# Forgetting attention and channel mix on one core: new durations for GpSimd's operations and a fixed part per matmul in the planner that orders the instructions

## The chip, the cores and the metric

The kernel runs on one core of one Trainium2 chip. The metric is device time in microseconds, the median over runs. A profiled execution lists every instruction of the five engines: TensorE (PE for its matmuls, PEld for its weight loads), VectorE (DVE), ScalarE (ACT), GpSimd (POOL) and SyncE (SP), which issues nearly all DMAs.

## The reference

Inputs: `q`, `k`, `v` of 8 batches x 8 heads x 576 positions x 64, a gate `s` per head and position, and the weights of a channel mix with `d_model` 512 and `d_ff` 1024. All is float32.

```python
scores = scale * np.matmul(q, k.transpose(0, 1, 3, 2))
cum = np.cumsum(np.maximum(s, 0.0), axis=-1)
bias = -(cum[:, :, :, None] - cum[:, :, None, :])
scores = np.where(causal, -1e9, scores + np.minimum(bias, 0.0))
attn = np.exp(scores - scores.max(-1, keepdims=True))
attn = attn / (attn.sum(-1, keepdims=True) + 1e-09)
x = np.matmul(attn, v)        # heads side by side: (8, 576, 512)
...
xk = mu_k * x + (1.0 - mu_k) * x_prev      # x_prev: x one position earlier
xr = mu_r * x + (1.0 - mu_r) * x_prev
k = np.maximum(xk @ w_k, 0.0)
out = 1 / (1 + np.exp(-(xr @ w_r))) * (k * k @ w_v)
```

## The kernel before, in words

**Attention.** The work goes in 36 visits, each a pair of heads of one batch: batch 0 in two parts (the first three query tiles, then the last two), the batches behind it whole, with four visits each. A visit takes, head by head: score products on TensorE (line 847 for the first 8 visits, in plain float32; line 858 afterwards, where q and k are split into a high and a low part and two products replace the plain one), written to one of two PSUM banks named `s`; a reduction on VectorE (line 875) that adds the causal mask, keeps the row minimum `nm` and writes the scores to `W`; the exponential on ScalarE (line 893) with the row sums in `sums`; on GpSimd a small operation on `rinv` (line 956), on VectorE the reciprocal (line 961); the normalizing on GpSimd (line 912). Then the probabilities are turned: in the first 12 visits by TensorE (lines 1001, 1016), later by 32x32 transposes on VectorE (line 939) and DMAs from `turned` to `ph` (line 1137). The product with v (`po`, lines 975 and 1166) ends a visit, and its result goes to `x_d` in DRAM. GpSimd also makes the split of q and k (`KH`, line 811; `G`, line 815).

**Channel mix.** The 4608 positions are cut into 18 chunks of 256. A chunk mixes x with its predecessor (ScalarE, line 1230; VectorE, line 1241, in the PSUM bank `xp`), splits the result into a high part (ScalarE, line 1261) and a low part `xl` (VectorE, line 1263), and multiplies: the hidden products with `w_k` (line 1308), the gate with `w_r` (line 1359) and the output with `w_v` (line 1390). They accumulate in one of two PSUM banks named `m`, which the eviction `g` on VectorE (line 1400) sets free at the end of an output. Chunk 0 multiplies in plain float32; afterwards each product is done three times (high x high, low x high, high x low).

**Weights.** They arrive as 64-bit floats, 20 blocks of 128 x 512. ScalarE and four operations on VectorE (lines 678, 685, 689, 696) convert a block, in the banks `m` and `xp`. The two banks `m` are given out in turn: first to the blocks of `w_k` and `w_r`, then to the hidden products of chunk 0 and what follows. On GpSimd a cast (line 709) and a subtraction (line 714) then split it into the high and low halves `wr_k`, `wr_r`, `wr_v`.

**What sets the order.** The program is first recorded as 7652 tasks (class `Plan`); then a planner orders them. Each task names its engine, a duration in ns, the buffers it reads and writes, and a due time. `Plan.forward` runs a list scheduling: of the tasks that are ready on an engine it takes the one with the earliest due time (on TensorE, VectorE and ScalarE out of the next few). `Plan.backward` gives new due times from the result; 40 such passes are made, and the order of the pass with the earliest planned end is written out, engine by engine. Inside an engine that order is fixed; between engines, semaphores hold it. While TensorE has nothing to do before the first chunk, `forward` puts in filler matmuls on the identity (line 447). The durations come from small helpers: `pe` for TensorE takes the columns times a rate, `pool` for GpSimd the elements per partition times a rate plus a constant `extra` that the caller gives (36 for a memset, 114 for the casts and the subtraction to `G`, 94 for line 714, 100 for line 956, 244 for line 912).

```python
def pe(emit, reads, writes, n, m=P, cycle=1.0625 / 2.4, k=P, land=None):
    i = plan.add("PE", n * cycle, emit, reads, writes, land=land or 0.83 * m + 1)
...
def pool(emit, reads, writes, n, extra, rate=0.8333):
    return plan.add("POOL", n * rate + extra, emit, reads, writes)
...
if name != "v":                       # load_weight: a block of w_k or w_r
    ps = bank(1, "m", 2)
...
return bank(1, "m", 2)                # product_bank: the sums of a chunk
...
order, _, _, emits = best
for n, i in enumerate(order):
    for emit in emits.get(n, ()):
        emit()
    self.tasks[i][2]()
```

Of the kernel before, what the change touches and what calls it, by code (L numbers as in the profile page):

```python
# [337 lines left out]
def forgetting_attention_then_channel_mix(  # L338
# [38 lines left out]
    plan = Plan()  # L377
# [13 lines left out]


    def pe(emit, reads, writes, n, m=P, cycle=1.0625 / 2.4, k=P, land=None):
        i = plan.add("PE", n * cycle, emit, reads, writes, land=land or 0.83 * m + 1)
        plan.columns[i] = n * k / P * (4 if cycle > 1 else 1)
        if m == 64 and n > 190 and cycle < 1:
            plan.spare.add(i)
        return i
# [27 lines left out]
    def dve(emit, reads, writes, n, rate=0.96, ports=None):  # L426
        i = plan.add("DVE", n / rate + 68, emit, reads, writes)
        plan.side(i, ports)
        return i

    def pool(emit, reads, writes, n, extra, rate=0.8333):
        return plan.add("POOL", n * rate + extra, emit, reads, writes)

    def aside(emit, reads, writes, ns):
        return plan.add("SP", 1, emit, reads, writes, land=1300 + ns)
# [86 lines left out]
    def blanks():  # L522
        u = turned_d.get()
        for h in range(2):
            a, step = slots(h, 0, 0), slots(h, 1, 1) - slots(h, 0, 0)
            pool(
                lambda a=a, step=step: nc.gpsimd.memset(
                    u[:, 2:4, a : a + step * (NQ - 1) + 1 : step], 0.0
                ),
                [], [(turned_d, (h, t)) for t in range(NQ)], 64 * NQ, 36,  # L530
            )
            pool(
                lambda a=a: nc.gpsimd.memset(u[64:P, 0:2, a : a + 1], 0.0), [], [(turned_d, (h, 0))], 64, 36,
            )

    def zero(t):
        for kb in range(NQ):
            pool(
                lambda kb=kb: nc.gpsimd.memset(t.get()[64:P, col(kb, P * kb) : col(kb, P * kb) + 64], 0.0),
                [], [(t, ("h", kb))], 64, 36,  # L540
            )
# [292 lines left out]
    def scores(b, h, tiles, blocks, G, G2, KH, KL):  # L834
# [7 lines left out]
        def products(t, m, i, k0, w, W):  # L842
            ps = bank(1, "s", 2)
            q0 = QS[t] - QS[tiles[0]]
            if G2 is None:
                pe(
                    lambda: nc.tensor.matmul(
                        ps.get()[:, :w],
                        G.get()[0:65, h % 2, q0 : q0 + P],
                        KH.get()[0:65, h % 2, k0 : k0 + w],  # L850
                        start=True,
                        stop=True,
                    ),
                    [(y, (h % 2, r)) for y in (G, KH) for r in range(2)], [ps], w, P, 4 / 2.4,
                )
            for x, (g, K) in enumerate(((G, KH), (G2, KL)) if G2 is not None else ()):
                pe(
                    lambda x=x, g=g, K=K: nc.tensor.matmul(  # L858
                        ps.get()[:m, :w],
                        g.get()[: 64 + PIECES if x else P, h % 2, q0 : q0 + m],  # L860
                        K.get()[: 64 + PIECES if x else P, h % 2, k0 : k0 + w],
                        start=x == 0,
                        stop=x == 1,
                    ),
                    [(g, (h % 2, 0)), (K, (h % 2, 0))]
                    + ([(g, 1), (K, (h % 2, 2))] if x else [(g, (h % 2, 1)), (K, (h % 2, 1))]), [ps], w, m,
                )
# [123 lines left out]
    def weighted(pts, V, xT, tiles, blocks, hp):  # L991


        def transposed(pt, ph):
# [3 lines left out]
            def turn(ps, place, t, k0, m):  # L998

                pe(  # L1000
                    lambda: nc.tensor.transpose(
                        ps.get()[0:m, place : place + P].bitcast(F32R),
                        piece(pt[t].at[0], pt[t].at[1] + lead(t) + k0, m),
                        ident_r.ap,
                    ),
                    [(pt[t], i) for i in range(3)] + [ident_r], [ps], P, m, land=TURN,
                )
# [618 lines left out]
```

## Time and profile before

| | us |
|---|---|
| median of 3 runs | 796.99 (794.56 to 801.29) |
| the profiled execution's own time | 794.9 |
| its span, first to last instruction | 793.1 |
| TensorE busy | 772.1 |
| VectorE busy | 556.1 |
| ScalarE busy | 467.8 |
| GpSimd busy | 344.2 |

The profiled execution is one run; the span is its time without what lies around the instructions. Matmuls are pipelined, and their recorded durations overlap, so busy time of TensorE says that there was a matmul under way and not that it ran at its peak; the distance from one matmul to the next says more. An idle time that a row shows in brackets is followed by the engine and line that ended it.

### The profile page before, as it was taken

To read this page: it belongs to the slowest core of one execution; us is meant where nothing else is said; L and a number is where in the kernel's file an instruction comes from. 1 tells how busy PE (TensorE), PEld (TensorE's weight loads), DVE (VectorE), ACT (ScalarE), POOL (GpSimd) and SP (SyncE) were. 2 spreads that over 40 slices of the span, in tenths; PEclk is the share of its full clock that TensorE was granted. 3 is DMA by queue.
4 is the path that set the end of the run, shared out by engine and by line. 5 is a ranking of instruction groups with operands and counts; after the bars stand their busy time and mean duration, and the time that the engine had idled before them with its cause. 6 is when DMAs were issued, how large, how long until landed. Compare 5 with 4: busy or idle time off the path is not lost.

```text
span 793.1 us, 15958 instructions
## 1 busy us (share of the span) xinstructions
PE 772.1 (97%) x5115; PEld 634.6 (80%) x5115; DVE 556.1 (70%) x1860; ACT 467.8 (59%) x1305; POOL 344.2 (43%) x616
## 2 busy tenths in 40 slices
PE   7989999999999999999999999999999999999998
PEld 5657767888787878788788888887888788888997
DVE  5989885578766877676687677768877787355521
ACT  3987887766654765474564567456655666345420
POOL 6748999743633444441344434343444421000000
PEclk8999999999999999999999999999999999999999
DMA  6898855688898998898689888889888776421000
GB/s 182 238 293 219 241 152 156 163 214 210 229 234 215 236 230 209 220 250 207 176 201 238 208 221 226 217 232 224 230 229 218 179 198 169 115 75 41 14 27 27
DMA packets 64068, 150.00 MB, mean 189 GB/s; under 512 B 14078, under 2 KB 25604, under 8 KB 63984
## 3 DMA queue, kind: packets, MB, share of 16 engines
q1 hardware_dynamic: 63824, 148.82, 72.6%
q8 instruction: 40, 0.66, 0.4%
q14 instruction: 44, 0.36, 0.1%
q10 hardware_dynamic: 160, 0.16, 0.1%
HBM read 50.29 MB, written 18.43 MB: 87 GB/s over the span
## 4 chain that ended last, share of the span: by engine, by line
PE 44%; DVE 14%; DMA 13%; SPq 11%; POOL 7%; ACT 5%; issue 5%; DVEq 0%; POOLq 0%; ACTq 0%
SPq L1137 11%; PE m L1308 11%; PE m L1390 9%; DMA ph<-turned 4%; DVE turned L939 4%; PE s L858 4%; DMA x<-x_d 4%; PE m L1359 4%; PE po L1166 3%; POOL W L912 3%; DVE W L875 3%; DVE xp L1241 3%; ACT xp L1230 2%; PE s L1390 2%; POOL G L815 2%
## 5 line engine op out<-in xcount | busy, mean ns | idle before, releaser
L893 ACT ACTIVATE W<-W,nm 128x448 f32<-128x448 f32 (+4 forms) x320 | 178.7, 559 | 71.8 <-DVE nm L875 68.2
L1308 PE MATMUL m<-xh,wr_k 128*128 128x256 f32 x960 | 185.1, 282 | 1.6 <-DVE g L1400 1.0
L912 POOL TENSOR_SCALAR W<-W,rinv 128x192 f32<-128x192 f32 (+4 forms) x320 | 164.6, 530 | 26.4 <-DVE rinv L961 24.9
L875 DVE CUSTOM_DVE_ANT_0 W<-s,causal 128x448 f32<-128x448 f32 (+5 forms) x320 | 129.6, 417 | 48.3 <-PE s L858 42.5
L1390 PE MATMUL m<-wr_v,kh 128*128 128x512 f32 (+1 forms) x480 | 159.4, 393 | 0.0
L1308 PEld LDWEIGHTS m<-xh,wr_k 128*128 128x128 f32 x960 | 153.6, 190 | 4.1 <-DVE kl L1345 1.5
L939 DVE STREAM_TRANSPOSE turned<-W 128x64 f32<-128x64 f32 (+5 forms) x432 | 121.9, 327 | 33.5 <-DMA ph<-turned 20.3
L1308 PE MATMUL m<-xl,wr_k 128*128 128x256 f32 x480 | 136.2, 284 | 0.0
L858 PE MATMUL s<-KH,G 128*64 128x64 f32 x336 | 105.0, 325 | 4.5 <-DVE nm L875 4.0
L956 POOL TENSOR_SCALAR rinv<-sums 128x5 f32<-128x5 f32 (+2 forms) x72 | 17.0, 236 | 212.9 <-ACT W L893 206.6
L1230 ACT ACTIVATE xp<-x,mu 128x256 f32<-128x256 f32 (+3 forms) x160 | 66.8, 417 | 67.0 <-DMA x<-x_d 39.7
L1390 PEld LDWEIGHTS m<-wr_v,kh 128*128 128x128 f32 x480 | 89.2, 188 | 15.1
L858 PE MATMUL s<-KL,G 67*64 67x64 f32 x336 | 98.3, 296 | 0.0
L1390 PE MATMUL m<-wr_v,kl 128*128 128x512 f32 (+1 forms) x240 | 94.1, 392 | 0.0
L1308 PEld LDWEIGHTS m<-xl,wr_k 128*128 128x128 f32 x480 | 91.4, 190 | 0.9
L1241 DVE SCALAR_TENSOR_TENSOR xp<-x,mu,xp 128x256 f32<-128x256 f32 (+3 forms) x160 | 64.8, 405 | 34.6 <-ACT xp L1230 32.4
L1359 PE MATMUL m<-wr_r,xh 128*128 128x512 f32 x240 | 81.4, 399 | 0.7 <-DVE kl L1345 0.6
L858 PEld LDWEIGHTS s<-KH,G 128*64 128x64 f32 x336 | 60.3, 180 | 23.3 <-DVE nm L875 14.3
L815 POOL TENSOR_TENSOR G<-raw,KH 128x1152 fp32r<-128x1152 f32 x28 | 74.6, 2665 | 1.8
L1166 PE MATMUL po<-ph,V 128*64 128x64 f32 (+4 forms) x768 | 67.2, 327 | 1.6 <-DMA ph<-turned 1.2
L858 PEld LDWEIGHTS s<-KL,G 67*64 67x64 f32 x336 | 60.4, 180 | 9.1 <-issue 3.0
L1166 PEld LDWEIGHTS po<-ph,V 128*64 128x64 f32 x768 | 39.7, 137 | 27.4 <-issue 23.3
(141 smaller groups left out, 1287.3 us busy)
## 6 DMA issues: line engine op xcount, KB each, us to landing
ph<-turned SPq DMA_DIRECT2D x384, 120.0 KB
raw<-in_q SPq DMA_DIRECT2D x28, 576.0 KB
G<-KH SPq DMA_DIRECT2D x56, 288.0 KB
V<-in_v SPq DMA_DIRECT2D x32, 320.0 KB
out<-g SPq DMA_DIRECT2D x35, 256.0 KB
x_d<-xT SPq DMA_DIRECT2D x28, 288.5 KB
KL<-G SPq DMA_DIRECT2D x28, 288.0 KB
KH<-KH SPq DMA_DIRECT2D x28, 288.0 KB
```

The source lines that it names most:

```text
L815: lambda: nc.gpsimd.tensor_tensor(out=G.get(), in0=x.get(), in1=f32(KH.get()), op=ALU.subtract),
L858: lambda x=x, g=g, K=K: nc.tensor.matmul(ps.get()[:m, :w], g.get()[: 64 + PIECES if x else P, h % 2, q0 : q0 + m], K.get()[: 64 + PIECES i ...
L875: lambda a=a, e=e, at=at, i=i: nc.vector.tensor_tensor_reduce(out=W.ap[:m, at : at + e - a], in0=ps.get()[:m, a - k0 : e - k0], in1=causal ...
L893: lambda: nc.scalar.activation(W.ap[:m, :n], W.ap[:m, :n], AF.Exp, bias=nm.get()[:m, 3 * t + mi : 3 * t + mi + 1], scale=-1.0, accum_out=s ...
L912: lambda: nc.gpsimd.tensor_scalar(out=to(), in0=W.ap[:m, :n], scalar1=rinv.get()[:m, t : t + 1], scalar2=1.0, op0=ALU.mult, op1=ALU.mult,),
L939: lambda a=a, e=e, g=g, n=n: nc.vector.transpose(at(a, e, g), W.ap[:m, P * a : P * a + n].rearrange("p (k g x) -> p k g x", g=g, x=32),),
L1137: lambda g=g, i=i: nc.sync.dma_start(across.get()[32 * g : 32 * g + 32, i], turned_d.get()[32 * i : 32 * i + 32, g]),
L1166: nc.tensor.matmul(to, V.get()[:, kb, j], x, start=ps is rest or kb == 0, stop=ps is rest or kb == NQ - 1 or t == NQ - 1, skip_group_check ...
L1241: lambda n=n, o=o, i=i, to=to: nc.vector.scalar_tensor_tensor(out=x_out.get()[:, c, o : o + n] if plain else to(), in0=x.get()[:, c, o + i ...
L1308: lambda u=u, f=f, c=c, n=n, y=y, x=x: nc.tensor.matmul(ps.get()[:, u * CT : (u + 1) * CT], y[:, f % 4 * P : (f % 4 + 1) * P], x.get()[:, ...
L1359: lambda c=c, n=n, x=x, y=y: nc.tensor.matmul(ps.get(), x.get()[:, c, ts], y, start=c == 0 and n == 0, stop=c == NC - 1 and n == products - 1,
L1390: lambda f=f, n=n, x=x, y=y, ps=ps, ms=ms: nc.tensor.matmul(ps.get()[:, :m], x.get()[:, f, ts], y[:, ms], start=f == 0 and n == 0, stop=f ...
```

## The change

The planner's duration of a matmul, of whatever size, gets 4.5 ns more, and four of the constants of GpSimd's operations are replaced by larger ones: 36 by 90, 94 by 140, 100 by 218, 114 by 165. The durations set nothing but the order.

```diff
@@ -391,7 +391,7 @@
-        i = plan.add("PE", n * cycle, emit, reads, writes, land=land or 0.83 * m + 1)
+        i = plan.add("PE", n * cycle + 4.5, emit, reads, writes, land=land or 0.83 * m + 1)
...
@@ -428,8 +428,10 @@
+    POOL_MORE = {36: 90, 94: 140, 100: 218, 114: 165}
+
     def pool(emit, reads, writes, n, extra, rate=0.8333):
-        return plan.add("POOL", n * rate + extra, emit, reads, writes)
+        return plan.add("POOL", n * rate + POOL_MORE.get(extra, extra), emit, reads, writes)
```

Lines behind 430 have a number larger by two afterwards. Three places of the new order follow, before and after each.

VectorE's queue before the first product of chunk 0, before the change. `w_r_2` and `w_k_3_1` are weight blocks, `m0` and `m1` the two PSUM banks in which they are converted, `W_0` and `W_1` the scores of the two heads, `nm` their row minima, `s0` and `s1` the score banks:

```order
L689 SCALAR_TENSOR_TENSOR m0_218<-w_r_2_0_128,m0_218 128x512
L875 ISA W_1_1024_576_82,nm1_241<-s1_213,causal_95,nm1_241 128x224
L875 ISA nm1_241 128x1
L696 SCALAR_TENSOR_TENSOR w_r_2_0_128<-w_r_2_0_128,m0_218 128x512
L875 ISA W_1_1024_576_82,nm1_241<-s1_213,causal_95,nm1_241 128x64
L875 ISA nm1_241 128x1
L678 TENSOR_SCALAR m1_401<-m1_401 128x512
L685 TENSOR_SCALAR m1_401<-m1_401 128x512
L961 RECIPROCAL rinv1_304<-rinv1_304 128x2
L689 SCALAR_TENSOR_TENSOR m1_401<-w_k_3_1_122,m1_401 128x512
L875 ISA W_0_576_448_76,nm0_226<-s0_216,causal_95 128x448
L875 ISA nm0_226 128x1
```

The same stretch of VectorE's queue after the change:

```order
L698 SCALAR_TENSOR_TENSOR w_k_3_1_122<-w_k_3_1_122,m1_248 128x512
L687 TENSOR_SCALAR m0_217<-m0_217 128x512
L877 ISA W_0_576_448_76,nm0_228<-s0_215,causal_95 128x448
L877 ISA nm0_228 128x1
L963 RECIPROCAL rinv1_305<-rinv1_305 128x2
L691 SCALAR_TENSOR_TENSOR m0_217<-w_r_2_0_128,m0_217 128x512
L877 ISA W_0_1024_576_77,nm0_228<-s1_213,causal_95 128x288
L877 ISA nm0_228 128x1
L680 TENSOR_SCALAR m1_248<-m1_248 128x512
L877 ISA W_0_1024_576_77,nm0_228<-s0_215,causal_95,nm0_228 128x224
L877 ISA nm0_228 128x1
L698 SCALAR_TENSOR_TENSOR w_r_2_0_128<-w_r_2_0_128,m0_217 128x512
```

The last step of `w_r_2` now stands behind `w_k_3_1` and behind three reductions of the next visit's scores.

GpSimd's queue where the low halves of the weights `wr_r` are made, before the change (`rinv0` belongs to head 0 of the visit, `W_0` is what is normalized with it):

```order
L838 MEMSET sums1_179 128x1
L714 TENSOR_TENSOR wr_r_0_0_125<-w_r_0_0_124,wr_r_0_0_125 128x512
L714 TENSOR_TENSOR wr_r_1_0_127<-w_r_1_0_126,wr_r_1_0_127 128x512
L1559 MEMSET xT0_763 128x1
L714 TENSOR_TENSOR wr_r_2_0_129<-w_r_2_0_128,wr_r_2_0_129 128x512
L956 TENSOR_SCALAR rinv0_273<-sums0_167 128x5
L709 CAST wr_v_1_0_135<-w_v_1_0_134 128x512
L838 MEMSET sums0_167 128x1
L714 TENSOR_TENSOR wr_r_3_0_131<-w_r_3_0_130,wr_r_3_0_131 128x512
L912 TENSOR_SCALAR W_0_64_192_74<-W_0_64_192_74,rinv0_273 128x192
L912 TENSOR_SCALAR W_0_256_320_75<-W_0_256_320_75,rinv0_273 128x320
L912 TENSOR_SCALAR W_0_576_448_76<-W_0_576_448_76,rinv0_273 128x448
```

The same stretch of GpSimd's queue after the change (`KH1` is the high part of the q and k of a later visit):

```order
L958 TENSOR_SCALAR rinv0_272<-sums0_168 128x5
L840 MEMSET sums1_180 128x1
L716 TENSOR_TENSOR wr_k_3_1_123<-w_k_3_1_122,wr_k_3_1_123 128x512
L914 TENSOR_SCALAR W_0_64_192_74<-W_0_64_192_74,rinv0_272 128x192
L914 TENSOR_SCALAR W_0_256_320_75<-W_0_256_320_75,rinv0_272 128x320
L914 TENSOR_SCALAR W_0_576_448_76<-W_0_576_448_76,rinv0_272 128x448
L914 TENSOR_SCALAR W_0_1024_576_77<-W_0_1024_576_77,rinv0_272 128x576
L914 TENSOR_SCALAR W_0_192_64_298<-W_0_0_64_73,rinv0_272 64x64
L840 MEMSET sums0_168 128x1
L711 CAST wr_v_1_0_135<-w_v_1_0_134 128x512
L813 CAST KH1_908<-raw1_154 128x1152
L716 TENSOR_TENSOR wr_r_0_0_125<-w_r_0_0_124,wr_r_0_0_125 128x512
```

The normalizing of head 0 moves ahead of all four `wr_r` blocks, the last of which stands 14 places later than before.

VectorE's queue at the end of a chunk (388 us in the trace of before), before the change. `g1` is the eviction that frees a bank `m`, `xp0` and `xl10` the mixing and the low part of the next chunk, `turned` the transposes of attention:

```order
L1263 TENSOR_TENSOR xl10_1364<-xp0_162,xh10_1356 128x512
L939 STREAM_TRANSPOSE turned_90<-W_1_576_448_81 128x3x4x32
L939 STREAM_TRANSPOSE turned_90<-W_1_1024_576_82 128x4x4x32
L1400 SCALAR_TENSOR_TENSOR g1_1195<-g1_1195,m0_218 128x512
L939 STREAM_TRANSPOSE turned_90<-W_1_256_320_80 128x2x32
L939 STREAM_TRANSPOSE turned_90<-W_1_576_448_81 128x2x32
L939 STREAM_TRANSPOSE turned_90<-W_1_1024_576_82 128x2x32
L1241 SCALAR_TENSOR_TENSOR xp0_162<-x0_1201,mu1_92,xp0_162 128x256 x2
```

The same place after the change:

```order
L1265 TENSOR_TENSOR xl10_1304<-xp0_161,xh10_1296 128x512
L1243 SCALAR_TENSOR_TENSOR xp0_161<-x0_1193,mu1_92,xp0_161 128x256 x2
L963 RECIPROCAL rinv1_305<-rinv1_305 128x5
L941 STREAM_TRANSPOSE turned_90<-W_1_64_192_79 128x4x32
L1265 TENSOR_TENSOR xl10_1304<-xp0_161,xh10_1296 128x512
L941 STREAM_TRANSPOSE turned_90<-W_1_0_64_78 64x2x32
L941 STREAM_TRANSPOSE turned_90<-W_1_64_192_79 128x2x32
L941 STREAM_TRANSPOSE turned_90<-W_1_256_320_80 128x2x4x32
L1402 SCALAR_TENSOR_TENSOR g1_1181<-g1_1181,m0_217 128x512
```

The two large transposes now follow the eviction, and the next mixing steps with their low part stand ahead of it.

## Rows read from the trace of the kernel before

**Rows 1.** The page: busy time, share and count of each engine.

```profile
PE 772.1 (97%) x5115; PEld 634.6 (80%) x5115; DVE 556.1 (70%) x1860; ACT 467.8 (59%) x1305; POOL 344.2 (43%) x616
```

**Rows 2.** Sums by stretch: length, busy (count) per engine, clock, DMA share, GB/s.

```profile
0.00:60.00 60.00, 52.18 (x296) 35.56 (x297) 49.60 (x173) 42.46 (x152) 36.00 (x94) 0.91 0.82 239
60.00:160.00 100.00, 99.20 (x637) 74.18 (x636) 73.61 (x264) 79.06 (x245) 90.43 (x132) 1.00 0.69 186
160.00:680.00 520.00, 511.42 (x3508) 429.00 (x3507) 388.03 (x1344) 306.23 (x827) 217.74 (x390) 1.00 0.85 215
```

**Rows 3.** Sums by stretch, two of the 20 us stretches.

```profile
40.00:60.00 20.00, 17.51 (x95) 11.11 (x96) 18.00 (x58) 16.17 (x52) 8.85 (x17) 0.91 0.96 296
...
380.00:400.00 20.00, 18.06 (x113) 16.37 (x112) 14.76 (x45) 11.22 (x28) 5.98 (x12) 0.91 0.69 181
```

**Rows 4.** The chain that ended last: start us, length us, what.

```profile
51.33 3.49 PE po L975 x20
...
63.42 1.89 PE po L975 x20
...
733.62 2.81 PE m L1308 x24
...
750.41 5.54 PE m L1390 x24
```

**Rows 5.** GpSimd's instructions by line: count, duration in ns as min/median/max.

```profile
L956 POOL TENSOR_SCALAR rinv<-sums x72: 223/236/253, 13.6 to 672.9; 128x5 f32<-128x5 f32 x56, 128x3 f32<-128x3 f32 x8, 128x2 f32<-128x2 f32 x8
...
L811 POOL CAST KH<-raw x28: 1134/1144/1151, 61.0 to 626.4; 128x1152 fp32r<-128x1152 f32 x28
...
L815 POOL TENSOR_TENSOR G<-raw,KH x28: 2628/2667/2690, 62.7 to 627.6; 128x1152 fp32r<-128x1152 f32 x28
...
L714 POOL TENSOR_TENSOR wr_k<-w_k,wr_k x8: 1272/1274/1290, 68.9 to 95.0; 128x512 fp32r<-128x512 f32 x8
```

**Rows 6.** Timeline before 60 us: start us, length us, engine, line, [idle before <-releaser].

```profile
18.45 1.27 PE L447 MATMUL xp<-ident 128*128 128x256 bf16 x10
...
51.17 0.68 DVE L696 SCALAR_TENSOR_TENSOR w_r<-w_r,m 128x512 int32<-128x512 int32 x1
...
56.02 0.60 PE L1308 MATMUL m<-xh,w_k 128*128 128x256 f32 x2
...
57.69 0.45 DVE L875 CUSTOM_DVE_ANT_0 W<-s,causal,nm 128x224 f32<-128x224 f32 x1 [0.67 <-PE s L847]
```

**Rows 7.** Timeline: the last low halves of two weights, and chunk 1's first readers.

```profile
95.05 1.29 POOL L714 TENSOR_TENSOR wr_k<-w_k,wr_k 128x512 fp32r<-128x512 f32 x1
...
103.81 1.29 POOL L714 TENSOR_TENSOR wr_r<-w_r,wr_r 128x512 fp32r<-128x512 f32 x1
...
127.78 0.35 PE L1308 MATMUL m<-xh,wr_k 128*128 128x256 f32 x1
...
154.52 0.39 PE L1359 MATMUL m<-wr_r,xh 128*128 128x512 f32 x1
```

**Rows 8.** Timeline of TensorE, 389 to 393 us.

```profile
389.53 0.39 PE L1308 MATMUL m<-xh,wr_k 128*128 128x256 f32 x1 [1.02 <-DVE g L1400]
...
392.45 0.74 PE L858 MATMUL s<-KH,G 128*128 128x448 f32 x1 [0.81 <-DVE nm L875]
```

**Rows 9.** Timeline of VectorE and ScalarE, 387 to 391 us.

```profile
387.18 0.65 DVE L1263 TENSOR_TENSOR xl<-xp,xh 128x512 fp32r<-128x512 f32 x1
387.76 1.14 DVE L939 STREAM_TRANSPOSE turned<-W 128x384 f32<-128x384 f32 x2
388.83 0.64 DVE L1400 SCALAR_TENSOR_TENSOR g<-g,m 128x512 f32<-128x512 f32 x1
...
387.86 0.99 ACT L1230 ACTIVATE xp<-x,mu 128x256 f32<-128x256 f32 x2 [0.77 <-DVE xl L1263]
...
390.81 0.59 ACT L1261 CAST xh<-xp 128x512 fp32r<-128x512 f32 x1 [1.96 <-DVE xp L1241]
```

**Rows 10.** Timeline of TensorE near 292 us.

```profile
292.68 0.42 PE L858 MATMUL s<-KH,G 128*128 128x320 f32 x1 [0.70 <-DVE nm L875]
```

## The prediction

> **What bounds the kernel now.** I read the page's busy line first, then the sums by stretch, then the time from one matmul to the next, then the waits that TensorE itself shows.
>
> TensorE is busy 772.1 us of 793.1 [rows 1]. By stretch the missing 21 us lie in three places [rows 2]: 7.8 us before 60 us (60.00 less 52.18), 0.8 us from 60 to 160, 8.6 us from 160 to 680. That leaves 3.8 us behind 680, most of it the last eviction and store. GpSimd is the fullest engine beside it, but in one stretch alone: 90.43 of 100 us from 60 to 160; afterwards it has 217.74 of 520 [rows 2].
>
> The clock is part of the bound. The granted clock was 0.91 in 40 to 60 and again in 380 to 400 [rows 3], which is 1.8 us of 20 lost each time, so a part of each stretch ran at 1.2 GHz in place of 2.4. What it does to one stage stands in two rows of the same 20 matmuls: 3.49 us at 51.33, 1.89 us at 63.42 [rows 4], so a fall costs about 1.6 us.
>
> A busy TensorE runs close to its rate: 24 matmuls of 256 columns took 2.81 us (117.1 ns each), 24 of 512 columns 5.54 us (230.8 ns) [rows 4]. The planner had 113.3 and 226.7 ns; with 4.5 ns more it has 117.8 and 231.2. So the new constant for TensorE is right within 1 ns, and the old one was 3 % short on the small ones. For GpSimd the traced medians are 236 ns (the small scalar operation on rinv), 1144 (cast to KH), 2667 (the subtraction to G), 1274 (the subtraction of a weight block) [rows 5]; the planner had 102 to 104, 1074, 2660, 1226 and now has 220 to 222, 1125, 2711, 1272. Three of these four come much nearer, G's goes from 7 ns short to 44 ns over.
>
> **The change part by part.** No instruction of the computation is added, removed or altered; the planner's list scheduling gives another order. About half of TensorE's instructions stand at another place, the largest move is 49 places, and what runs behind 695 us stands in the same order on every engine. On TensorE 8 of 75 filler matmuls on the identity go, a count from the two orders. So the sum is one of waits, made against the profiled execution's own 794.9 us.
>
> *Fillers.* Ten of them took 1.27 us at full clock [rows 6], so eight are 1.0 us. They stand in the first 30 us, where TensorE waits for VectorE anyway, so part of this turns into waiting. Bounds −1.0 and 0; I take −0.5.
>
> *The start of the channel mix.* The first product of chunk 0 writes to a PSUM bank that the conversions of the weight blocks use before it; on that bank the block w_r_2 is last. Before, its last step began at 51.17 and took 0.68, and the product came at 56.02 behind other work [rows 6]. In the new order that step stands behind the conversion of w_k_3_1 and three score reductions, the last of which began at 57.69 in the trace of before, after a wait of 0.67 for TensorE [rows 6]; the bank then comes free near 58.7, or near 58.0 without that wait. The product is thus 2.0 to 2.7 us late. The cover is TensorE's own: score products and transposes of the next visits now stand ahead of it. Bounds −1.0 (that work, started sooner, also saves waits) and +2.7 (no cover); nearest to the covered case, since in the row of 56.02 the product already took turns with that work, +0.4.
>
> *GpSimd from 66 to 148 us.* The normalizing of probabilities and the splits of q and k move ahead of the low halves of the weights. The last wr_k low half began at 95.05, the last wr_r one at 103.81; their readers, chunk 1's products, began at 127.78 (wr_k) and 154.52 (wr_r) [rows 7], so delays of about 5 and 10 us are hidden by 30 and 50 us of slack. The gain is bounded by TensorE's whole idle time there, 0.8 us [rows 2], a loss would need a delay of 30 us or more. Bounds −0.8 and 0, I take −0.2.
>
> *The bank at the chunk starts, at 388 us.* TensorE waited 1.02 us at 389.53 for the eviction g on VectorE, and 0.81 us at 392.45 for a reduction behind it [rows 8], and the clock fell there [rows 3]. VectorE's eviction ran at 388.83 behind two transposes of 1.14 us together [rows 9]. In the new order it loses these two, but the next two mixing steps and their subtraction (xl) stand ahead of it. With the times of before: subtraction done at 387.83; ScalarE's two steps 387.86 to 388.85; the two mixing steps end near 389.35; ScalarE's cast (0.59) lets the second subtraction start near 390.0; it and three small transposes take 1.35; the eviction would end at 392.0 instead of 389.47. That is +2.5 us; upstream, four transposes (0.9 us) leave the front of the chain, so less is likelier. Bounds −1.0 (the wait goes) and +2.5 (nothing upstream helps); I take +1.0. Queued behind this eviction are transposes and score reductions of attention, whose products stand among other work of TensorE.
>
> *One wait that is filled.* At 292.68 the score product waits 0.70 us for VectorE [rows 10]. Three output products stood between it and the scores before; now five do. Two more are 0.46 us; bounds −0.7 and 0, taken −0.5.
>
> *The other waits from 160 to 680*, 8.6 less 1.0, 0.8 and 0.7, or about 6 us, are drawn anew. A truer TensorE duration tells the planner that results of other engines come earlier in terms of matmuls, so readers move closer to their producers: less cover. Truer GpSimd durations move its readers away: more cover. I take 0, with half of the 6 us on either side.
>
> The sum is −0.5 + 0.4 − 0.2 + 1.0 − 0.5 = +0.2, or 795.1 us on the profiled execution. The three runs shown have a median 2.1 us above that execution (796.99, from 794.56 to 801.29), so no change would read as 795.9, halfway, for this forecast and the rivals; with +0.2 that is 796. About 1 %, 8 us, is what a measurement of this kernel can tell from no change.
>
> **The clock, for and against.** The rows show a fall at 0.91 in 380 to 400, where TensorE was still busy 18.06 of 20 us and its longest recorded waits were 1.02 and 0.81 us [rows 3, 8]. The Trainium skill (TensorE: Matmul & The Clock Gate, section "What's actually happening") says that the lower clock is the default, that activity lifts it and that an idle stretch lets it fall; this speaks against removing fillers. By the strict form of that rule, waits of about 1 us would never bring a fall, and the slower case below would lose its clock part of 1.6; the trace disagrees, as the fall at 392 stands behind such waits alone.
>
> **Rivals.** *The truer numbers pay everywhere.* Half of the 8.6 us from 160 to 680 goes (4.3), the fall near 392 with it (1.6), and a third of the 7.8 us before 60 (2.6): −8.5, or 787.4. For it speaks that GpSimd is the fullest engine from 60 to 160 and that its small operation on rinv was planned at less than half of its 236 ns [rows 5]. Against it: GpSimd's stage costs TensorE 0.8 us only, and of the two waits shown in [rows 8] both are for VectorE, whose durations do not change. Chance 0.17.
>
> *Slower: evictions late at the chunk starts.* The mechanism is the one at 388 us, at several places. In the new order eleven evictions before 600 us have more of VectorE's work ahead of them than before, by 0.1 to 1.6 us at the traced durations, and eleven have less. If three of them cost what the worked case has as its upper end (2.5) and one more clock fall joins (1.6) they give +9.1, or 805. It decides where the eviction comes later than the products of the bank before it last, 24 of 117 ns or 2.8 us. Against it: only one such wait of TensorE stands out before. Chance 0.14.
>
> *The change does not do what it says.* The order behind 160 us is close to the old one, so the waits stay as they are, with the fillers alone gone: 795.4. This lies inside the forecast's band and I give it 0.24; the forecast proper has 0.45.
>
> **How the numbers follow.** Faster by over 1 % (under 788) is the first rival, 0.17; slower by over 1 % (over 804) the second, 0.14; the rest is 0.69. The range reaches from the first rival's value, 787, to 804, just short of the second's: it leaves out half of the first rival's chance below and most of the second's above, about 0.2 in all. The forecast's own bounds, −1.0 − 1.0 − 0.8 − 1.0 − 0.7 − 3.0 and +2.7 + 2.5 + 3.0, make −7.5 and +8.2 if all fell one way, 788 to 804, which lies in the same range.
>
> **What would show it.** Right: TensorE busy near 771 us and its idle time from 160 to 680 still 6 to 11 us; first product of chunk 0 at 57 to 59 us; the wait at the score product near 292 under 0.3 us; an eviction wait of over 1.5 us near 389. GpSimd's durations within 2 % of the old ones and 90 us busy again in 60 to 160. Wrong: an idle time of TensorE from 160 to 680 under 4.5 us or over 14, one clock fall more or one less than the two of [rows 3], or a chunk 1 that waits for wr_k or wr_r.

## The result and the profile after

The changed kernel took 803.65 us (median of 20 runs, 798.98 to 814.85) beside 797.89 us for the kernel before on the same chips (20 runs, 790.24 to 806.84). The ratio is 1.0087, 95% interval 1.0063 to 1.0112: slower by 7 us by this ratio, by 5.8 between the medians. The forecast of 796 and no change was wrong, though the time lies just inside its range. Twenty runs resolve a quarter of a per cent here; the 1 per cent that the prediction took as the limit was too coarse.

The profiled execution after is one of the quickest of the new kernel, as the one before was of the old: 798.98 us, span 797.2 against 793.1. Its busy line and its sums by stretch (length, busy and count per engine, clock, DMA share, GB/s), with the stretch behind 680 us:

```profile
PE 772.1 (97%) x5107; PEld 632.4 (79%) x5107; DVE 561.1 (70%) x1860; ACT 467.5 (59%) x1305; POOL 344.5 (43%) x616
```

```profile
0.00:60.00 60.00, 52.21 (x298) 34.82 (x299) 53.35 (x183) 44.84 (x160) 38.89 (x98) 0.94 0.77 236
60.00:160.00 100.00, 100.00 (x644) 75.04 (x643) 74.90 (x263) 76.74 (x239) 90.81 (x134) 1.00 0.70 191
160.00:680.00 520.00, 507.37 (x3457) 424.38 (x3457) 387.01 (x1331) 305.50 (x823) 214.71 (x384) 0.99 0.85 213
680.00:798.00 118.00, 112.54 (x714) 98.16 (x710) 45.82 (x86) 40.46 (x84) 0.10 (x1) 1.00 0.18 50
```

TensorE is busy for the same 772.1 us as before [rows 1]. Beside [rows 2] its idle time is unchanged before 60 us (7.8), falls by 0.8 from 60 to 160 (to nothing), rises by 4.0 from 160 to 680 (from 8.6 to 12.6) and by 0.8 behind that (117.2 less 112.54, against 3.8). That is +4.0, and the spans differ by 4.1. So what these two executions show of the loss lies in the steady stage, as waits of TensorE; of the 7 us of the ratio they show 4.1. The waits that it shows itself from 160 to 680 us (who waits, for whom: us, times, longest), first of the kernel before, then after:

```profile
PE s L858 <- DVE nm L875: 4.0, 8, 0.9
PE m L1308 <- DVE g L1400: 1.0, 1, 1.0
...
PE m L1308 <- DVE kl L1345: 0.6, 3, 0.2
```

```profile
PE s L860 <- DVE nm L877: 8.8, 13, 1.8
PE m L1310 <- DVE kl L1347: 1.8, 3, 0.8
```

A score product (s) that waits until VectorE has reduced (nm) the scores that its bank held before: 4.0 us became 8.8. The wait for an eviction (g) is gone. The longest of these waits, in TensorE's timeline after:

```profile
293.16 0.42 PE L860 MATMUL s<-KH,G 128*128 128x320 f32 x1 [1.85 <-DVE nm L877]
...
341.56 0.25 PE L860 MATMUL s<-KH,G 128*64 128x64 f32 x1 [0.97 <-DVE nm L877]
...
381.81 0.40 PE L860 MATMUL s<-KH,G 128*128 128x288 f32 x1 [1.36 <-DVE nm L877]
...
502.44 0.42 PE L860 MATMUL s<-KH,G 128*128 128x320 f32 x1 [1.08 <-DVE nm L877]
...
503.31 0.47 PE L860 MATMUL s<-KH,G 128*128 128x448 f32 x1 [0.32 <-DVE nm L877]
...
536.61 0.42 PE L860 MATMUL s<-KH,G 128*128 128x320 f32 x1 [0.55 <-DVE nm L877]
...
661.59 0.41 PE L860 MATMUL s<-KH,G 128*128 128x320 f32 x1 [0.96 <-DVE nm L877]
```

Why the reduction is late stands in VectorE's own queue. In front of the first of these waits, in the timeline of VectorE:

```profile
290.67 0.96 DVE L1243 SCALAR_TENSOR_TENSOR xp<-x,mu,xp 128x256 f32<-128x256 f32 x2
292.29 0.69 DVE L1265 TENSOR_TENSOR xl<-xp,xh 128x512 fp32r<-128x512 f32 x1 [0.65 <-ACT xh L1263]
292.89 0.20 DVE L877 CUSTOM_DVE_ANT_0 W<-s,causal 64x64 f32<-64x64 f32 x1
```

and the score product that this reduction reads, in TensorE's:

```profile
289.59 0.19 PE L860 MATMUL s<-KH,G 128*64 128x64 f32 x1
```

The scores were there before 290 us. The reduction came at 292.89, behind two mixing steps and the subtraction xl, for which VectorE stood 0.65 us idle until ScalarE's cast was done. The order inside an engine's queue is fixed, so a ready reduction waits behind a mixing chain that is not. At 381 us the picture is the same; at 341 and 661 us it is a mixing step alone, for which VectorE stood idle for 1.64 and 0.91 us until ScalarE's part of it was done; at 502 it is transposes and a subtraction.

Behind 40 us the clock fell twice again, at other places: not in 40 to 60 or 380 to 400, as in [rows 3], but here:

```profile
40.00:60.00 20.00, 17.95 (x103) 11.98 (x104) 19.91 (x63) 17.65 (x56) 10.85 (x20) 1.00 0.87 275
340.00:360.00 20.00, 18.84 (x134) 15.50 (x133) 16.09 (x59) 14.55 (x42) 9.63 (x16) 0.91 0.85 217
380.00:400.00 20.00, 18.64 (x127) 16.89 (x127) 15.50 (x49) 11.83 (x31) 7.88 (x15) 1.00 0.66 170
500.00:520.00 20.00, 18.60 (x118) 15.43 (x118) 12.95 (x47) 8.15 (x25) 7.57 (x12) 0.91 0.81 199
```

Some executions run disturbed, on whatever kernel; the ratios leave them out, and as the profiles of e2, e7 and e13 are of such executions, their rows are not compared.

### The profile page after: what moved, and what is told of

It reads as the page before. It is cut to its first block, busy times and chain, and to the rows that moved or that the text cites. A ratio compares the mean times of both kernels' runs of the same rounds, so it can differ in the third digit from the quotient of the medians.

```text
span 797.2 us, 15944 instructions
## 1 busy us (share of the span) xinstructions
PE 772.1 (97%) x5107; PEld 632.4 (79%) x5107; DVE 561.1 (70%) x1860; ACT 467.5 (59%) x1305; POOL 344.5 (43%) x616
## 4 chain that ended last, share of the span: by engine, by line
PE 52%; SPq 12%; DVE 11%; DMA 11%; ACT 7%; issue 4%; POOL 3%; DVEq 0%; POOLq 0%; ACTq 0%
PE m L1310 14%; SPq L1139 11%; PE m L1392 11%; PE s L860 6%; PE m L1361 4%; DMA x<-x_d 4%; DVE turned L941 4%; PE po L1168 3%; DVE xp L1243 2%; ACT xp L1232 2%; ACT W L895 2%; PE po L977 2%; PE s L1392 2%; DMA KH<-KH 2%; DVE xl L1265 2%
## 5 line engine op out<-in xcount | busy, mean ns | idle before, releaser
L1392 PE MATMUL m<-wr_v,kh 128*128 128x512 f32 (+1 forms) x480 | 161.2, 398 | 0.0
L860 PE MATMUL s<-KL,G 67*64 67x64 f32 (+1 forms) x336 | 99.2, 299 | 0.0
L860 PEld LDWEIGHTS s<-KL,G 67*64 67x64 f32 (+1 forms) x336 | 61.0, 182 | 9.2 <-issue 3.2
L1322 ACT ACTIVATE r<-m 128x512 f32<-128x512 f32 x64 | 38.1, 595 | 40.9 <-PE m L1310 37.7
```

What stands on the lines that cost most here:

```text
L860: lambda x=x, g=g, K=K: nc.tensor.matmul(ps.get()[:m, :w], g.get()[: 64 + PIECES if x else P, h % 2, q0 : q0 + m], K.get()[: 64 + PIECES i ...
L1392: lambda f=f, n=n, x=x, y=y, ps=ps, ms=ms: nc.tensor.matmul(ps.get()[:, :m], x.get()[:, f, ts], y[:, ms], start=f == 0 and n == 0, stop=f ...
```

## The experiments

All ratios are to the kernel before, run beside it on the same chip. The diff of e4 is against the kernel before, all others are against the changed kernel. A changed number makes the planner give another order; such an order is called a draw here. Three theories at first: the longer matmul costs (1), GpSimd's numbers cost (2), any redraw of the order costs or gains by chance (3).

**The two halves alone.** e1 is the change without GpSimd's numbers, e2 the change without the matmul's.

```diff
-    POOL_MORE = {36: 90, 94: 140, 100: 218, 114: 165}
+    POOL_MORE = {}
```

> The kernel before with the 4.5 ns per matmul alone; GpSimd's durations as in the kernel before. Theory 1 (the longer matmul in the plan is what costs; readers of VectorE's results are placed with nothing to spare): as slow as the whole change, a ratio to before of 1.006 to 1.012, TensorE idle from 160 to 680 us 11 to 14 us (before 8.6, after 12.6). Theory 2 (GpSimd's numbers do it): 0.997 to 1.003 and 7 to 10 us. Theory 3 (any new number draws the order anew, the sign is chance): anywhere from 0.993 to 1.012, with waits at other places than in the changed kernel.

```diff
-        i = plan.add("PE", n * cycle + 4.5, emit, reads, writes, land=land or 0.83 * m + 1)
+        i = plan.add("PE", n * cycle, emit, reads, writes, land=land or 0.83 * m + 1)
```

> The kernel before with GpSimd's new durations alone; the matmul as in the kernel before. Theory 1: no loss behind 160 us, a ratio of 0.995 to 1.002 (the start may keep the 3 us that the changed kernel had won by then). Theory 2: 1.006 to 1.012, with 11 to 14 us of idle TensorE from 160 to 680. Theory 3: anywhere from 0.993 to 1.012.

Measured: e1 1.0204 (1.0153 to 1.0256), twice the loss of the whole change; e2 1.0006 (0.9964 to 1.0049). Theory 2 falls. Of e1 the sum of the steady stage, and the largest single wait met in this study, on four engines:

```profile
160.00:680.00 520.00, 494.97 (x3364) 415.38 (x3363) 374.95 (x1296) 297.55 (x801) 213.15 (x381) 0.99 0.85 209
```

```profile
540.00 0.59 SPq L1424 DMA_DIRECT2D x<-x_d  x1
540.63 6.34 SPq L1139 DMA_DIRECT2D ph<-turned  x10
```

```profile
544.26 0.78 ACT L1232 ACTIVATE xp<-x,mu 128x192 f32<-128x192 f32 x2 [5.35 <-DMA x<-x_d]
```

```profile
545.07 0.42 DVE L1243 SCALAR_TENSOR_TENSOR xp<-x,mu,xp 128x192 f32<-128x192 f32 x1 [4.43 <-ACT xp L1232]
545.98 0.29 DVE L1243 SCALAR_TENSOR_TENSOR xp<-x,mu,xp 128x64 f32<-128x64 f32 x1 [0.49 <-ACT xp L1232]
546.18 0.21 DVE L877 CUSTOM_DVE_ANT_0 W<-s,causal 64x64 f32<-64x64 f32 x1
```

```profile
546.45 0.63 PE L860 MATMUL s<-KH,G 128*128 128x320 f32 x1 [5.69 <-DVE nm L877]
```

Read from the top: SyncE issues the load of x at 540.00; ScalarE mixes at 544.26 when it has landed; VectorE has stood idle for 4.43 us with its mixing step at the head of its queue; the reduction behind that starts at 546.18, and TensorE, which has waited 5.69 us for it, goes on. TensorE is idle for 25.0 us of the 520.

**The late reductions moved ahead.** e3 keeps the changed kernel's order but for nine reductions (task numbers of the plan: what is moved, and in front of what); a merge of the engines' queues writes the instructions.

```diff
+    MOVES = ((3122, 2580), (3126, 2580), (4020, 3232), (4174, 3471), (4178, 3471),
+             (5651, 5174), (5655, 5174), (6867, 6326), (6871, 6326))
...
         order, _, _, emits = best
+        order = self.moved_up(order)
```

> The changed kernel's own order, with nine score reductions moved ahead in VectorE's queue at five places (near 291, 340, 380, 501 and 660 us), in front of the mixing steps, the subtraction or the transposes behind which they stood; every other engine's order is untouched. The waits of TensorE in front of score products there are 1.85, 0.97, 1.36, 1.08 with 0.32, and 0.96 us, 6.5 us together, and the clock fell behind two of them. If these waits are the loss: 4 to 7 us less than the changed kernel, a ratio to before of 0.999 to 1.004, and both falls of the clock gone. If the lost time is only passed on (the mixing comes later and TensorE waits for it instead): 1.007 to 1.011, as the changed kernel.

Measured: 1.0041 (1.0009 to 1.0073), between the two expectations; its interval overlaps that of the changed kernel, so in time up to half of the loss may have come back. The profiled execution shows none of that. The same places, some 5 us later in this execution:

```profile
298.80 0.40 PE L882 MATMUL s<-KH,G 128*128 128x288 f32 x1 [1.57 <-DVE nm L899]
...
347.64 0.36 PE L882 MATMUL s<-KH,G 128*128 128x192 f32 x1 [2.74 <-DVE nm L899]
...
508.24 0.40 PE L882 MATMUL s<-KH,G 128*128 128x288 f32 x1 [0.76 <-DVE nm L899]
...
540.25 0.41 PE L882 MATMUL s<-KH,G 128*128 128x320 f32 x1 [1.89 <-DVE nm L899]
...
668.22 0.40 PE L882 MATMUL s<-KH,G 128*128 128x288 f32 x1 [0.25 <-DVE nm L899]
```

The wait near 381 is gone, those near 502 and 661 are shorter by 0.6 and 0.7, but the one at 341 grew from 0.97 to 2.74, and the one near 537, at which nothing was moved, from 0.55 to 1.89. In sum these are 7.2 us against 7.1. At 347 us VectorE stood idle with a mixing step at the head of its queue, and the next reduction stood behind that:

```profile
346.08 1.07 DVE L1265 SCALAR_TENSOR_TENSOR xp<-x,mu,xp 128x64 f32<-128x64 f32 x3 [2.74 <-ACT xp L1254]
347.06 0.51 DVE L899 CUSTOM_DVE_ANT_0 W<-s,causal,nm 128x288 f32<-128x288 f32 x1
```

So in this execution the lost time is passed on along VectorE's queue; whether repairing single places returns a part of it in time stays open.

**Redraws that carry no knowledge.** e4, e5 and e18 change the old matmul by a tenth or two of a nanosecond, with GpSimd's old numbers.

```diff
-        i = plan.add("PE", n * cycle, emit, reads, writes, land=land or 0.83 * m + 1)
+        i = plan.add("PE", n * cycle + 0.1, emit, reads, writes, land=land or 0.83 * m + 1)
```

> A control: the kernel before with 0.1 ns per matmul, a number that carries no knowledge, but moves 1317 of TensorE's instructions by up to 43 places. Theory 1 and theory 2: as before, 0.997 to 1.003, idle from 160 to 680 us 7 to 10 us. Theory 3: off by as much as the change itself, 0.5 per cent or more either way, or an idle time outside 7 to 10 us.

e5 has `n * cycle - 0.1`:

> A second control: the kernel before with 0.1 ns taken from each matmul. If a redraw without any knowledge costs about what the first control showed (1.0048, TensorE idle 14.5 us of 160 to 680): 1.002 to 1.010 and 11 to 16 us, which would mean that the order before was a good draw and that any redraw loses. If the first control was itself an unlucky draw: 0.996 to 1.001 and 7 to 10 us.

and e18, run last, `n * cycle + 0.2`:

> The kernel before with 0.2 ns per matmul: no knowledge, another draw. If the longer planned matmul costs as such: in the band of the old matmul, 0.988 to 1.005, waits for VectorE's reductions from 160 to 680 us 3 to 7 us (the six so far have 3.4 to 6.4). If it is the draw alone: as likely 1.006 to 1.016 with 8 us or more.

Measured: 1.0048 (1.0011 to 1.0085), 0.9882 (0.9798 to 0.9967) and 0.9994 (0.9961 to 1.0027). So a number without meaning can move this kernel by half a per cent up or a whole one down, or not at all: theory 3 holds as far as that. e5 is the quickest order of the study, faster than both kernels; it is taken for a lucky draw and not for a better number, as −2.25 and −4.5 ns below gain nothing.

**The matmul's number by its dose.** e6 and e17 are the whole change with 4.4 and 4.6 ns, e7 the matmul alone with 4.4, e9, e10 and e11 the matmul alone with −4.5, −2.25 and +2.25.

```diff
-        i = plan.add("PE", n * cycle + 4.5, emit, reads, writes, land=land or 0.83 * m + 1)
+        i = plan.add("PE", n * cycle + 4.4, emit, reads, writes, land=land or 0.83 * m + 1)
```

> The changed kernel with 4.4 in place of 4.5 ns per matmul: the same knowledge, another draw (1920 of TensorE's instructions stand elsewhere than in the changed kernel). If the change's loss is a property of its numbers: 1.006 to 1.012 and 11 to 14 us of idle TensorE from 160 to 680. If it is the luck of a draw: anywhere from 0.995 to 1.02, with waits at other places.

> The matmul alone, with 4.4 ns in place of 4.5. The first such run had 1.0204 and 25.0 us of idle TensorE from 160 to 680. If the longer matmul without GpSimd's numbers is bad as such: 1.015 to 1.025 and 20 us or more again. If that was an unlucky draw: 1.002 to 1.010 and 11 to 16 us, as the controls.

> The kernel before with 4.5 ns taken from each planned matmul, a number that is 8 ns wrong. Theory 1 by its dose (a planned matmul that is too short makes the results of the other engines look late, so their readers are put further back, and this hidden reserve is what the true number removes): faster than before, 0.985 to 0.997, with 5 to 8 us of idle TensorE from 160 to 680. Theory 3 (each draw by itself): anywhere from 0.988 to 1.015, no order along the dose.

> The kernel before with 2.25 ns taken from each planned matmul. Theory 1 by its dose: between the kernel before and the one with 4.5 ns less, 0.988 to 1.000, idle 5 to 9 us from 160 to 680. Theory 3: anywhere from 0.988 to 1.015.

> The kernel before with half of the change's TensorE part, 2.25 ns more for each planned matmul. Theory 1 by its dose: half of what 4.4 and 4.5 ns gave (1.0176 and 1.0204), that is 1.005 to 1.012, idle 11 to 17 us from 160 to 680. Theory 3: anywhere from 0.988 to 1.015.

> The changed kernel with 4.6 ns per matmul in place of 4.5. If the longer planned matmul costs as such: in the band of its family, 1.006 to 1.016, waits for VectorE's reductions from 160 to 680 us 8 to 19 us (the seven so far have 8.1 to 18.5). If it is the draw alone: as likely 0.99 to 1.005 with 3 to 7 us.

All of them beside the controls; the last column is the wait of score products for VectorE's reductions from 160 to 680 us (the row shown above of before and after), idle is 520 less TensorE's busy time there:

```
ns per matmul   GpSimd  other edit           ratio (95%)              idle   wait
-4.5  (e9)      old                          1.0007 (0.9955-1.0059)   12.1    4.3
-2.25 (e10)     old                          1.0012 (0.9971-1.0053)    9.1    4.6
-0.1  (e5)      old                          0.9882 (0.9798-0.9967)    5.3    3.9
 0    (before)  old                          1                         8.6    4.0
 0    (e2)      new                          1.0006 (0.9964-1.0049)     -      -
+0.1  (e4)      old                          1.0048 (1.0011-1.0085)   14.5    6.4
+0.2  (e18)     old                          0.9994 (0.9961-1.0027)    6.8    3.8
+2.25 (e11)     old                          1.0137 (1.0057-1.0217)   13.9   13.3
+4.4  (e7)      old                          1.0176 (1.0076-1.0276)     -      -
+4.5  (e1)      old                          1.0204 (1.0153-1.0256)   25.0   18.5
+4.4  (e6)      new                          1.0088 (1.0047-1.0129)   17.0   14.1
+4.5  (after)   new                          1.0087 (1.0063-1.0112)   12.6    8.8
+4.6  (e17)     new                          1.0160 (1.0097-1.0224)   11.3    8.2
+4.5  (e8)      new     mixing +55/+40 ns    1.0088 (1.0046-1.0131)   13.1   10.6
+4.5  (e12)     new     VectorE +120 ns      1.0147 (1.0066-1.0228)   13.7    8.7
```

Two families that do not touch, as long as SyncE keeps its old number (of four kernels with another one, which follow below, three do not fit): six kernels with −4.5 to +0.2 ns lie at 0.988 to 1.005 (mean 0.999), eight with +2.25 to +4.6, two of them with a further edit told below, at 1.009 to 1.020 (mean 1.014). Where the wait for reductions can be compared it is 3.8 to 6.4 us in the one and 8.2 to 18.5 in the other; the idle time overlaps. The means of these waits differ by 7.2 us, where 1.4 per cent are some 11 us, so they are most of the loss and not all of it. e17 and e18 were named with their bands before they ran, and both came out inside, e17 at the upper edge of its own. So beside SyncE's old number the longer matmul costs about 1.4 per cent on the mean, and a single draw scatters by about half a per cent around its family. Idle time and waits are those of one execution and do not give the ratio one by one. e17 has a low idle time and one of the highest ratios; in its profiled execution the granted clock was 0.53 from 40 to 60 us, and the first product of chunk 0 came at 69.18 us, against 55.76 in that of the changed kernel:

```profile
40.00:60.00 20.00, 19.48 (x76) 11.87 (x74) 14.31 (x44) 13.57 (x48) 7.86 (x19) 0.53 0.65 214
```

Three pairs of longer matmuls differ by GpSimd's numbers alone: e1 and the changed kernel (1.0204 and 1.0087), e7 and e6 (1.0176 and 1.0088), and e14 and e13 below (1.0145 and 1.0050). Each time GpSimd's new numbers give back about 1 per cent, some 8 us, while on the old matmul they give nothing (e2). The difference of two draws scatters by nearly as much, so three pairs make this likely and do not prove it.

The matmul's number has no dose on both sides: shorter than the old number gains nothing. e9 shows what it meets there, in the same list of waits:

```profile
PE m L1310 <- ACT xh L1263: 4.4, 2, 2.5
PE s L860 <- DVE nm L877: 4.3, 5, 1.5
```

Products of the channel mix now wait for the mixed input itself.

**Is a neighbour's number the cause?** If a true matmul hurts, another number may still be false. Three were tried. e8: the mixing steps.

```diff
-                    [source, (mu, which)], [(xm, (y, o)), (xm, "a")], n, 160, ports="S>P",
+                    [source, (mu, which)], [(xm, (y, o)), (xm, "a")], n, 200, ports="S>P",
...
-                    [(x_out, (c, o))] if plain else [(xm, (y, o)), (xm, "d")], n, ports=...
+                    [(x_out, (c, o))] if plain else [(xm, (y, o)), (xm, "d")], n + 53, ports=...
```

> The changed kernel with the mixing steps also set to what the trace shows: on VectorE 55 ns more for each (its shortest distance from one such step of 256 columns to the next instruction is 389 ns, the plan has 335), on ScalarE 40 ns more (411 against 373); the other operations of both engines are planned within 20 ns or so. Theory 4: a true matmul only hurts because the mixing steps, behind which the late score reductions stand in VectorE's queue, are planned too short; with them true the idle time of TensorE from 160 to 680 falls to 9 us or less and the ratio to 0.996 to 1.002. If it is a matter of the draw: 1.002 to 1.012 and 11 to 16 us, as the controls.

e12: more time between VectorE's results and their readers.

```diff
-    AFTER = {"PE": 235.0, "ACT": 150.0, "DVE": 160.0, "POOL": 60.0, "SP": 1000.0}
+    AFTER = {"PE": 235.0, "ACT": 150.0, "DVE": 280.0, "POOL": 60.0, "SP": 1000.0}
```

> The changed kernel with the reserve put back by name: the plan hands on each result of VectorE 120 ns later (280 in place of 160). If the lost reserve behind VectorE is the cause: the waits for VectorE's reductions fall (8.8 us of them from 160 to 680 in the changed kernel) to 5 us or less, the idle time to 9 us or less, the ratio to 0.994 to 1.002. If not: 1.004 to 1.013, as the changed kernel, or worse, as every reader is put further back.

Both stay in the slower family (table): theory 4 and the reserve behind VectorE fall. Then SyncE: in the row above ten issues of ph took 6.34 us, 634 ns each, where the plan has 520. e13 is the changed kernel with that, e14 the longer matmul alone, e15 the kernel before, e16 is e13 with the load of x 600 ns later.

```diff
-        return plan.add("SP", max(520, ns), emit, reads, writes, land=1300)
+        return plan.add("SP", max(634, ns), emit, reads, writes, land=1300)
```

> The changed kernel with every DMA issue planned at 634 ns at least, in place of 520: in the trace the issues of the turned probabilities follow one another every 634 ns (352 pairs, 624 to 645). Theory 5 (the true matmul hurts because SyncE is still planned too fast, so that the load of x, the mixing steps behind it and the score reductions queued behind those come later than planned): the waits for VectorE's reductions from 160 to 680 us fall from 8.8 to 5 us or less, the idle time from 12.6 to 9 or less, ratio to before 0.985 to 1.001. If SyncE's number is not the cause: 1.005 to 1.013, as the changed kernel and its neighbour.

> The longer matmul alone (GpSimd's old numbers), with DMA issues planned at 634 ns. Without the 634 it had 1.0204 (and 1.0176 at 4.4 ns). Theory 5: at least 1 per cent better than that, 0.990 to 1.007, waits for VectorE's reductions under 8 us (18.5 before this edit). If not the cause: 1.013 to 1.025.

> The kernel before (old matmul, old GpSimd numbers) with DMA issues planned at 634 ns. Theory 5: the old short matmul had hidden most of SyncE's error, so little is won: 0.988 to 1.003, waits for VectorE's reductions 2 to 5 us. If a longer issue alone decides, whatever the matmul: the same as the changed kernel with 634, within 0.4 per cent.

> As e13, and the load of x is planned to land 600 ns later (the plan has 4.24 us from the issue of a full load to the first mixing step, the trace 4.68 at 281.21 us and 5.04 at 369.37). Theory 5: as e13 or up to 0.5 per cent better; mixing steps no longer stand in front of VectorE's reductions waiting. If only the row of issues matters: as e13 within 0.4 per cent.

Measured: 1.0050 (1.0006 to 1.0093), 1.0145 (1.0063 to 1.0226), 1.0151 (1.0053 to 1.0250) and 1.0021 (0.9977 to 1.0066). The lists of waits from 160 to 680 us, of e14 and then of e15:

```profile
PE m L1310 <- ACT xh L1263: 5.8, 2, 4.5
PE s L860 <- DVE nm L877: 4.3, 6, 1.3
```

```profile
PE m L1308 <- DVE kl L1345: 6.7, 7, 2.5
PE s L858 <- DVE nm L875: 3.8, 5, 1.5
```

The wait for reductions did fall, in e14 from e1's 18.5 us to 4.3, as theory 5 wanted. But other waits took its place: products wait for mixed input that comes late (xh, 4.5 us at once), or in e15 for the low halves kl. On the old matmul the truer issue time even costs 1.5 per cent. So theory 5 falls for the longer matmul alone. For the whole change it stays open: 1.0050 and 1.0021 lie below all eight kernels of the slower family, e16 by 0.7 per cent, which is more than the scatter of a draw; yet in e16's profiled execution the idle time is 10.0 us and the wait for reductions 6.0, where theory 5 wanted 9 and 5 at most. And with 634 ns the two families do not part: the old matmul has 1.0151, the longer one 1.0145, 1.0050 and 1.0021. As far as four draws can tell, what the longer matmul costs hangs on SyncE's number.

**What stays open.** That the longer planned matmul leads to slower orders is shown over eight draws against six, with SyncE's issues at 520 ns and not with 634; why the planner then makes them is not shown. Excluded as the single cause are GpSimd's numbers, VectorE's handover and the mixing steps; the five worst places and SyncE's issues may be a part of it. One reading fits but was not tried: up to a common factor, a plan whose matmul is 2 to 4 per cent short is a plan in which every other engine and handover is 2 to 4 per cent long. The old number would then be a reserve spread over all engines at once, and each of e8, e12 and e13 put it back at one engine alone. The row from the matmul alone (1.0204) over GpSimd's numbers with it (1.0087) to SyncE's as well (1.0050, 1.0021) goes that way, one draw each; the mixing steps (e8, 1.0088) do not.

## Why the prediction was wrong, point by point

- *What bounds the kernel.* Right: TensorE is busy 772.1 us in both, GpSimd's durations did not move (235 ns on rinv against 236 in [rows 5]), it is busy 90.81 us from 60 to 160, and the change is one of waits.
- *The step that failed* is the last term, "The other waits from 160 to 680 ... I take 0, with half of the 6 us on either side". The sentence ahead of it named the mechanism with its right sign, less cover for readers of other engines' results when the matmul gets longer, and then set it off in full against GpSimd's truer numbers, without a price for either. The runs price both: the matmul alone costs +14 to +16 us (e7, e1; 1.0176 and 1.0204 of 798), and GpSimd's numbers, as the three pairs suggest, give back 7 to 9 of that, and nothing by themselves (e2). So the offset has the sign that the prediction gave it and about half the size, and +7 us is left where the term has 0. On the profiled execution the idle time outside the places priced apart went from the 6 us of the term to 10.8 (12.6 less the 1.85 at 293), +4.7, beyond the 3 that the term allowed; the waits for reductions rose by 4.8 in all.
- *The bank at 388 us*, +1.0 taken: wrong in sign. The subtraction stood ahead of the eviction, as the order had it:

```profile
388.30 0.65 DVE L1265 TENSOR_TENSOR xl<-xp,xh 128x512 fp32r<-128x512 f32 x1
...
389.48 0.64 DVE L1402 SCALAR_TENSOR_TENSOR g<-g,m 128x512 f32<-128x512 f32 x1
```

  but TensorE shows no wait from 386 to 396, where [rows 8] had 1.02 and 0.81, and the fall of the clock there is gone. The subtraction was done by 388.95, where the working had it start near 390, and TensorE itself came to this place later, as it had already waited at 341 and 381 us.
- *The wait at 292 us*, −0.5 taken: wrong. Two more output products stood in front of the score product, but the reduction was later still: 0.70 us in [rows 10] became 1.85. Counting what is ahead of the reader is half of it; what is ahead of the producer on its engine counts as much.
- *The start*, +0.4 taken, and *the fillers*, −0.5: not to be told. The first product of chunk 0 came at 55.76 us, not at 57 to 59, but e3 has the same instructions up to 290 us, and there it came at 60.59. Idle time before 60 us is the same to a tenth.
- *GpSimd from 66 to 148 us*, −0.2 taken: −0.8, the bound. Nothing in chunk 1 waited for wr_k or wr_r.
- *The rivals.* The slower case had the right time (805) for the wrong reason: it put the loss on evictions at chunk starts, whose wait went away. That truer numbers pay everywhere was refuted by e1. That the old order is just kept behind 160 us was refuted by the waits, and the redraws show that its price, 795.4, had no ground: of three numbers without meaning two moved the time, by 0.5 and 1.2 per cent, and it had allowed for 0.5 us.
- *What would show it.* 12.6 us of idle time from 160 to 680 lie outside the 6 to 11 called right, and short of the 14 called wrong; the number of clock falls stayed at two, though both moved.

## What to carry to other kernels

A planner's cost table that is nearer to the trace need not give a better order: correcting one engine's number alone can make it worse, and what it does depends on the numbers beside it. That the false number had been the plan's reserve is a reading that fits, and not more. Before a change of order is judged, redraw the order with a number that means nothing: here that alone moved the time by −1.2 to +0.5 per cent, and only a family of draws on each side (six against eight) showed a difference of 1.4, and that for one setting of SyncE's number. When a score product waits for a reduction, read the producer's queue from its head: the culprit is the instruction that stands there waiting for something else.

## What was not expected of the hardware

The start of the program differs between executions of the same instructions. e3's first 290 us are instruction for instruction those of the changed kernel; its row for 40 to 60 us, beside the one of after shown above:

```profile
40.00:60.00 20.00, 18.70 (x80) 11.03 (x80) 15.99 (x50) 14.21 (x46) 8.04 (x16) 0.66 0.73 251
```

The granted clock was 0.66 there against 1.00, and the first product of chunk 0 came 4.8 us later (60.59 against 55.76). A term of a few us before 60 us cannot be read from one profiled execution.

The length of a recorded wait does not tell whether the clock falls behind it. After the wait of 1.85 us at 293 the clock stayed up, after 0.97 us at 341 it fell:

```profile
280.00:300.00 20.00, 18.15 (x109) 13.57 (x108) 14.61 (x53) 11.89 (x32) 7.59 (x15) 1.00 0.85 209
```

The Trainium skill (TensorE: Matmul & The Clock Gate, section "What's actually happening") lets an idle stretch bring the lower clock. The trace agrees in that both falls stand behind waits, of 0.97 us and of 1.08 and 0.32; but TensorE was busy for 18.84 and 18.60 of the 20 us around them, so these are gaps and hardly a stretch, and no run here shows which waits do it.
